# Sums of seven products built up in PSUM, with ScalarE copying between the products

## The chip, the cores and the metric

The kernel runs on one core of a Trainium2 chip. A core has a matrix engine (TensorE, in the profile PE, with its weight loads as PEld), three engines for elementwise work (VectorE as DVE, ScalarE as ACT, GpSimd as POOL), a queue engine (SyncE as SP) and 16 DMA engines. Matrix products land in PSUM, in banks of 128 partitions by 512 float32; everything else lives in SBUF. Each engine works through its own queue in order, and engines wait for one another by semaphores.

The metric is the time of one execution on the device in microseconds, as the median of the runs. Lower is better.

## The reference

x is 2048 x 512. It is normalised per row, and two branches use it:

```python
    x = A_x
    xn = _layernorm(x, axis=-1)
    s = _A_ref(xn, A_wqkv, A_wo)
    g = _silu(_B_ref(xn, B_w1, B_b1, B_w2, B_b2))
    return x + s * g
```

Branch A is attention with 32 heads of 16 channels: `qkv = x @ wqkv` (512 x 1536), then each position attends to 8 positions at distances 0, 2, ..., 14 behind it, with a softmax over the 8, and `@ wo` (512 x 512). Branch B is `relu(x @ w1 + b1) ** 2 @ w2 + b2` with 1792 hidden channels. Everything is float32.

## The kernel before

**Precision.** A float32 product is made of three passes in a faster format: each operand is split into a high and a low part, and high x high, high x low and low x high are added in PSUM (`PASSES`). ScalarE makes the high parts (`high`), VectorE or GpSimd the low ones (`low`). A product of 128 rows with a 256-deep half of the weights is thus 6 matmuls of 128 x 512, a full 512-deep projection 12.

**Stages.** The first stage takes the 16 tiles of 128 rows in pairs. It loads and normalises x, transposes it, splits it (`xt`), projects it to q, k and v and stores these to DRAM (`sq`, `sk`, `sv`). The second stage takes four chunks of 512 rows and, for each, the 14 slices of the hidden layer (`up`, `down`), with the output product of the attention (`out_product`) in between. The attention itself (products `pr` and `pv` with reductions) runs on VectorE beside both stages, as a stream of small steps that the function `pump` hands out.

**Order of the work.** Every engine keeps the order in which the program text calls it. A planner's clock counts priced work of PE and VectorE; `pump(margin)` issues attention steps while VectorE's clock stays below PE's plus a margin, and `not_before(t)` moves VectorE's clock forward where an operation is expected to wait. In the first stage, `plan` lists for each pair of tiles and each of six steps the preparation of later pairs (transposes, high and low parts, statistics, normalisation, loads), and `beside(a, step)` issues that step's list and then pumps.

**The pairs of seven products.** For the tile pairs starting at 4, 6, 8, 10 and 12 (`SEVEN`), q and k of both tiles a and b are computed from seven half-depth products in place of eight (a scheme of the Strassen and Winograd kind). With sums `S[a, 0..3]` of halves of x (made by `sums`, split by `high_sums` and `low_sums`) and sums T1 to T4 of weights, the products are called here by their weights:

- Q0 (first half of tile a), Q1 (second half of a), T1, T2, T3 (with S0, S1, S2), K1 (with S3), T4 (second half of b);
- q of a = Q0 + Q1; u2 = Q0 + T2; u3 = u2 + T3; q of b = u3 + T4; k of a = u2 + T1 + K1; k of b = u3 + T1.

`pair_of_seven(a)` issues them. Each product goes to a PSUM buffer of its own (`psA`, tag "acc", four banks shared with the v projections `qkv(·, 2)`). ScalarE copies two of them (Q0 and T1) into the staging tiles `stg` of q and k; VectorE adds the other five to `stg` straight from PSUM, and GpSimd makes two more additions from SBUF. Then `store_qkv` sends k and q to DRAM on SP's queue. In the profile these products are `pm`, the projections `pq`; nearly all instructions carry the line 87 of a recording helper.

Of the kernel before, what the change touches and what calls it, by code (L numbers as in the profile page):

```python
# [8 lines left out]
F32 = mybir.dt.float32  # L9
FR = mybir.dt.float32r  # L10
AF = mybir.ActivationFunctionType
# [3 lines left out]
P = 128  # L15
# [15 lines left out]
GR = 8  # L31
CH = D // GR
# [7 lines left out]
Q0, Q1, K0, K1, V0, V1, T1, T2, T3, T4 = range(10)  # L40
# [11 lines left out]
MATMUL, TRANSPOSE, DVE_FIXED, SHARED, SLACK, LATE, ROOM0, ROOM = 227, 150, 150, 200, 500, 3000, 500, 3500  # L52
# [5 lines left out]
def body(ctx: ExitStack, tc: tile.TileContext, x, wqkv, wo, w1, b1, w2, b2, out):  # L58
# [3 lines left out]
    clock = {"PE": 0.0, "V": 0.0}  # L62
# [28 lines left out]
    PE, V, A, G = Ordered(nc.tensor, "PE"), Ordered(nc.vector, "V"), Ordered(nc.scalar), Ordered(nc.gpsimd)  # L91

    def not_before(t):
        clock["V"] = max(clock["V"], t)
# [3 lines left out]
    def queue(out, in_):  # L98

        tc.keep_in_program_order(dma(out, in_))  # L100
# [10 lines left out]
    def psA(name):  # L111
        return psum.tile([P, 512], F32, name=name, tag="acc", bufs=4)
# [21 lines left out]
    px, pstg, pxT = (p1ctx.enter_context(tc.tile_pool(name=n, bufs=1)) for n in ("px", "pstg", "pxT"))  # L134
# [17 lines left out]
    def buffer(name, i):  # L152
        return wts.tile([P, 2, 2, 512], FR, name=name, tag=f"b{i}")


    wq = [buffer(f"wq{i}", i) for i in range(10)]
# [213 lines left out]
    def pump(margin=-SLACK):  # L370

        limit = clock["PE"] + margin
        flush(clock["PE"])
        while True:
            if coming[0] is None:
                coming[0] = next(stream, None)
            if coming[0] is None or clock["V"] + coming[0] > limit:
                break
            coming[0] = next(stream, None)
        if coming[0] is None:  # L380
            not_before(limit)
# [11 lines left out]
    def next_w():  # L393

        f = len(w12)
        if f < NF:
            w12[f] = buffer(f"w{f}", HOME[f]) if f in HOME else p2.tile([P, 2, 2, 512], FR, name=f"w{f}")
            for i, r in enumerate(raws.pop(f)):
                split(w12[f][:, 0, i], w12[f][:, 1, i], r, G)
            if f + 2 < NF:  # L400
                load_w(f + 2)
# [3 lines left out]
    mv, means, rs, shifts, xn, xb, pTs, xt, xT, seen, Sf, Sp = ({} for _ in range(12))  # L405
# [122 lines left out]
    def part_x(t, h):  # L528
        return lambda p, i: xt[t][:, p, 2 * h + i]

    def part_s(a, j):
        return lambda p, i: Sp[a, j // 2][:, p, j % 2, i]

    def product(a, n, lhs, w):

        ps = psA(f"pm{a}_{n}")
        k = 0
        for i in range(2):
            for p, q in PASSES:
                PE.matmul(ps, lhs(p, i), wq[w][:, q, i, :], start=k == 0, stop=k == 5)  # L540
                k += 1
        return ps.rearrange("p (g c) -> p g c", g=GR)

    def new_stg(t, s):
        stgs[s] = pstg.tile([P, GR, 2, CH], F32, name=f"stg{t}_{s}", tag="stg", bufs=4)

    def qkv(t, s, between=None, late=False):

        ps = psA(f"pq{t}_{s}")
        order = [(kt, a, b) for kt in range(KT) for a, b in PASSES]  # L550
        if late:
            order.sort(key=lambda o: o[1])
        for n, (kt, a, b) in enumerate(order):
            PE.matmul(ps, xt[t][:, a, kt], wq[2 * s + kt // 2][:, b, kt % 2, :], start=n == 0, stop=n == 11)
            if between and n == 5:
                between()
        evacuate(t, s, ps)

    def evacuate(t, s, ps):
        if t % 2 == 0:  # L560
            new_stg(t, s)
        A.activation(stgs[s][:, :, t % 2], ps.rearrange("p (g c) -> p g c", g=GR), AF.Copy)
        if t % 2:
            store_qkv(t, s)

    def store_qkv(t, s):
        r0 = (t - 1) * P + (0 if s == 0 else HALO)
        dst = (sq, sk, sv)[s][:, r0:r0 + UP, :].rearrange("g (p e) c -> p g (e c)", e=2)
        queue(dst, stgs[s].rearrange("p g e c -> p g (e c)"))
        done = done_tiles["qkv"[s]]  # L570
        done[0] = t + 1
        done[1][t // 2] = clock["PE"]
# [8 lines left out]
    def up(c, f):  # L581
        ph = psH(f"ph{c}_{f}")
        n = 0
        for kt in range(KT):
            for a, b in PASSES:
                PE.matmul(ph.rearrange("p (j n) -> p j n", n=P), w12[f][:, a, 0, kt * P:(kt + 1) * P],
                          xT[c][:, :, b, kt, :], start=n == 0, stop=n == 11)
                n += 1
        if f == NF - 1 and c + 1 < NCH:
            load_xT(c + 1)  # L590
        h = hpool.tile([P, 2, 512], FR, name=f"h{c}_{f}", tag="h", bufs=3)
        A.activation(ph, ph, AF.Relu, bias=b1t[:, f:f + 1])
        A.activation(h[:, 0], ph, AF.Square)

        pool = c or f < 2 or f > 11
        full = hpool.tile([P, 512], F32, name=f"hf{c}_{f}", tag="hf") if pool else ph
        A.activation(full, ph, AF.Square)
        if pool:
            G.tensor_sub(h[:, 1], full, h[:, 0].bitcast(F32))
        hs[f] = h, None if pool else ph, clock["PE"] + 2000  # L600

    def lowh(f):
        h, ph, t = hs[f]
        if ph is not None:
            not_before(t)
            V.tensor_sub(h[:, 1], ph, h[:, 0].bitcast(F32))
# [29 lines left out]
    ps = psA("pq0_1")  # L636
# [10 lines left out]
    stats(2)  # L647
    clock.update(PE=12000.0, V=12500.0)
    qkv(1, 1, None, True)
    lows(0, 2)  # L650
    norm(2)
    stats(3)
    constants()
    qkv(0, 0, lambda: highs(2, 0))
    trans(2)
    lows(2, 0)
    norm(3)
    stats(4)
    qkv(1, 0, lambda: highs(2, 2))
    trans(3)  # L660
    lows(2, 2)
# [38 lines left out]
    for a in range(2, NT, 2):  # L700
        n, t = (2 if a < 6 else 0), a + 2
# [29 lines left out]
    def beside(a, step):  # L731

        for f, args in plan.get((a, step), ()):
            f(*args)
        for n in range(ahead.get((a, step), 0)):
            next_w()
        pump(LATE)
# [15 lines left out]
    def pair_of_seven(a):  # L753

        b, last = a + 1, a + 2 == NT
        new_stg(a, 1)
        new_stg(a, 0)
        q, k = stgs[0], stgs[1]
        p = product(a, 1, part_x(a, 0), Q0)
        A.activation(q[:, :, 0], p, AF.Copy)  # L760
        p = product(a, 5, part_s(a, 0), T1)
        A.activation(k[:, :, 1], p, AF.Copy)
        beside(a, 0)
        p = product(a, 6, part_s(a, 1), T2)
        not_before(clock["PE"])
        V.tensor_add(k[:, :, 0], q[:, :, 0], p)
        p = product(a, 2, part_x(a, 1), Q1)
        beside(a, 1)
        not_before(clock["PE"])
        V.tensor_add(q[:, :, 0], q[:, :, 0], p)  # L770
        p = product(a, 7, part_s(a, 2), T3)
        not_before(clock["PE"])
        V.tensor_add(q[:, :, 1], k[:, :, 0], p)
        G.tensor_add(k[:, :, 0], k[:, :, 0], k[:, :, 1])
        G.tensor_add(k[:, :, 1], k[:, :, 1], q[:, :, 1])
        p = product(a, 3, part_s(a, 3), K1)
        beside(a, 2)
        qkv(a, 2)
        not_before(clock["PE"] - 12 * MATMUL)
        V.tensor_add(k[:, :, 0], k[:, :, 0], p)  # L780
        store_qkv(b, 1)
        beside(a, 3)
        p = product(a, 4, part_x(b, 1), T4)
        beside(a, 4)
        not_before(clock["PE"])
        V.tensor_add(q[:, :, 1], q[:, :, 1], p)
        store_qkv(b, 0)
        if last:
            for f in range(2):
                up(0, f)  # L790
                pump()
            lowh(0)
        qkv(b, 2)
        beside(a, 5)

    for a in range(2, NT, 2):
# [89 lines left out]
    for c in range(NCH):  # L886
# [4 lines left out]
        for f in range(2, NF):  # L891
# [6 lines left out]
            if c == 0 and f in (3, 6):  # L898

                i = f // 6  # L900
# [65 lines left out]
        else:  # L966
# [13 lines left out]
            for j in range(2, TPC):  # L980
                n = D // 2 if j == TPC - 1 else D
# [25 lines left out]
```

## Time and profile before

| | |
|---|---|
| runs, us | 492.69, 496.27, 496.73 |
| median, us | 496.27 |
| span of the profiled execution, us | 487.2 |
| TensorE busy, mean granted clock | 481.0 us (99%), 1.000 |
| VectorE, ScalarE, GpSimd busy | 437.9 us (90%), 220.0 us (45%), 242.7 us (50%) |
| HBM traffic over the span | 160 GB/s |

The profile is of one execution; only its span, from the first to the last instruction, is given, and the run times include what lies before and after it. Times in it are microseconds from the start of the span unless marked ns. The window of the pairs of seven products is from 42 to 119 us. Where a row of instructions ends in "<-", the engine stood idle before it until the named engine and tile released it. Matmuls overlap their neighbours, so the duration of one (389 ns) is longer than the distance between two.

### The profile page before, as it was taken

What the parts mean: (1) busy time and instruction counts of PE and PEld (TensorE: products, weight loads), DVE (VectorE), ACT (ScalarE), POOL (GpSimd) and SP (SyncE); (2) the same over time, 40 slices, a digit from 0 to 9 for tenths busy, and PEclk for the clock granted to TensorE, in tenths of its full rate; (3) what the DMA queues carried; (4) which work ended last, traced back from release to release, by engine and by line L of the source; (5) the groups of instructions that cost most, each with busy time, mean ns of one, the idle gap of its engine ahead of it and who ended that gap; (6) DMA issues with size and microseconds to landing.
All of it is one profiled execution on the core that took longest, in us unless ns stands there. A gap on an engine that the chain in (4) does not pass through costs nothing.

```text
span 487.2 us, 5957 instructions
## 1 busy us (share of the span) xinstructions
PE 481.0 (99%) x2124; PEld 395.4 (81%) x2124; DVE 437.9 (90%) x369; ACT 220.0 (45%) x392; POOL 242.7 (50%) x178
## 2 busy tenths in 40 slices
PE   8999999999999999999999999999999999999996
PEld 5887788888888888888888888888888888888886
DVE  5987999999999997999999999999999999989234
ACT  5556386523454657336612432652233366223331
POOL 1325244044657869367546426784643488352210
PEclk9999999999999999999999999999999999999999
DMA  8899999879938998274618337371924755030322
GB/s 281 219 249 278 302 289 278 215 210 315 289 87 221 264 194 229 77 233 76 170 45 209 82 64 262 60 200 31 226 48 85 248 93 152 16 108 23 86 86 88
DMA packets 65530, 81.47 MB, mean 167 GB/s; under 512 B 6108, under 2 KB 49372, under 8 KB 64732
## 3 DMA queue, kind: packets, MB, share of 16 engines
q1 hardware_dynamic: 61180, 54.87, 40.6%
q10 hardware_dynamic: 4320, 26.22, 21.3%
q8 instruction: 17, 0.28, 0.3%
q14 instruction: 13, 0.11, 0.1%
HBM read 50.60 MB, written 27.32 MB: 160 GB/s over the span
## 4 chain that ended last, share of the span: by engine, by line
PE 96%; DVE 1%; issue 1%; DMA 1%; POOL 0%; ACT 0%; POOLq 0%
PE pb L87 31%; PE ph L87 31%; PE pq L87 15%; PE pm L87 9%; PE pw L87 9%; DVE pr L87 1%; DMA x<-in_A_x 1%; PE pxT L87 0%; POOL stg L87 0%; DVE z L87 0%; ACT xn L87 0%; DVE Sf L87 0%; DVE st L87 0%; ACT S L87 0%; DVE stg L87 0%
## 5 line engine op out<-in xcount | busy, mean ns | idle before, releaser
L87 PE MATMUL pb<-w,h 128*128 128x512 f32 x672 | 160.6, 389 | 0.0
L87 PEld LDWEIGHTS pb<-w,h 128*128 128x128 f32 x672 | 126.1, 188 | 26.2
L87 POOL TENSOR_TENSOR h<-hf,h 128x512 fp32r<-128x512 f32 x46 | 83.8, 1822 | 104.4 <-ACT hf L87 95.3
L87 PE MATMUL ph<-xU,w 128*128 128x512 f32 x504 | 120.6, 389 | 0.0
L87 PEld LDWEIGHTS ph<-xU,w 128*128 128x128 f32 x504 | 94.6, 188 | 19.6
L87 ACT ACTIVATE ph<-ph,b1t 128x512 f32<-128x512 f32 x56 | 36.9, 659 | 136.8 <-PE ph L87 135.5
L87 DVE TENSOR_TENSOR pr<-k,q 128x2048 f32<-128x2048 f32 x32 | 81.4, 2543 | 0.6
L87 DVE TENSOR_TENSOR pv<-v,L 128x2048 f32<-128x2048 f32 x32 | 79.0, 2468 | 2.5 <-POOL L L87 2.0
L87 DVE TENSOR_REDUCE L<-pr 128x128 f32<-128x2048 f32 x32 | 73.2, 2286 | 0.9
L87 DVE TENSOR_REDUCE v<-pv 128x256 f32<-128x2048 f32 x32 | 73.0, 2281 | 0.8
L87 PE MATMUL pw<-wot,oT 128*128 128x512 f32 (+1 forms) x204 | 45.9, 376 | 0.0
L87 PE MATMUL pq<-wq,xt 128*128 128x512 f32 x192 | 45.5, 389 | 0.0
L87 PEld LDWEIGHTS pw<-wot,oT 128*128 128x128 f32 x204 | 36.8, 188 | 7.1
L87 PEld LDWEIGHTS pq<-wq,xt 128*128 128x128 f32 x192 | 36.0, 188 | 7.5
L87 PE MATMUL ph<-xT,w 128*128 128x512 f32 x168 | 40.3, 389 | 0.0
L87 PEld LDWEIGHTS ph<-xT,w 128*128 128x128 f32 x168 | 31.5, 188 | 6.5
L87 ACT ACTIVATE h<-ph 128x512 fp32r<-128x512 f32 x56 | 33.7, 601 | 1.8
L87 ACT ACTIVATE stg<-pq 128x512 f32<-128x512 f32 x28 | 16.6, 597 | 39.5 <-PE pq L87 39.5
L87 POOL TENSOR_TENSOR w<-w1r,w 128x512 fp32r<-128x512 f32 x14 | 25.6, 1830 | 16.0 <-ACT w L87 15.6
L87 ACT ACTIVATE hf<-ph 128x512 f32<-128x512 f32 x46 | 27.3, 594 | 8.9 <-POOL h L87 8.9
L87 PE MATMUL pq<-wq,xT 128*128 128x512 f32 x132 | 30.9, 393 | 0.0
L87 PE MATMUL pm<-wq,S 128*128 128x512 f32 x120 | 29.7, 394 | 0.3 <-ACT S L87 0.3
(82 smaller groups left out, 505.1 us busy)
## 6 DMA issues: line engine op xcount, KB each, us to landing
k<-sk ACTq DMA_DIRECT2D x8, 960.0 KB, 7.9
v<-sv ACTq DMA_DIRECT2D x8, 960.0 KB, 8.2
sx<-xt SPq DMA_DIRECT2D x12, 512.0 KB, 5.6
xU<-sx ACTq DMA_DIRECT2D x6, 1024.0 KB, 7.9
x<-in_A_x SPq DMA_DIRECT2D x16, 256.0 KB, 5.2
sk<-stg SPq DMA_DIRECT2D x8, 512.0 KB, 4.9
sq<-stg SPq DMA_DIRECT2D x8, 512.0 KB, 5.7
sv<-stg SPq DMA_DIRECT2D x8, 512.0 KB, 5.7
```

Source lines behind the costliest of these rows:

```text
L87: return tc.keep_in_program_order(f(*a, **k))
```

## The change

The sums are no longer formed by VectorE. Three PSUM buffers are taken at the start of a pair: `sums_ps`, `first` and `five`.

- `sums_ps` receives Q0. Then T2, T3 and T4 are accumulated into it, so that it holds Q0, u2, u3 and q of b in turn. ScalarE copies it after each: to the PSUM buffer `first`, to a new SBUF tile `u2`, to the q tile of b (u3) and again to the q tile of b.
- `first`, which holds the copy of Q0, has Q1 accumulated into it and is copied out as q of a.
- `five` receives T1, is copied to the k tile of b, and has K1 accumulated into it.
- VectorE keeps one addition, k of a = u2 + `five`; GpSimd keeps one, k of b += u3.

The order of the products changes from Q0, T1, T2, Q1, T3, K1, v of a, T4, v of b to Q0, T1, v of a, T2, Q1, first half of v of b, T3, K1, second half of v of b, T4. The planned steps 0 to 5 move with it; step 3 and the store of k now come in the middle of v of b, and q is stored last.

```diff
-    def product(a, n, lhs, w):
-        ps = psA(f"pm{a}_{n}")
+    def product(ps, lhs, w, start=True):
         k = 0
         for i in range(2):
             for p, q in PASSES:
-                PE.matmul(ps, lhs(p, i), wq[w][:, q, i, :], start=k == 0, stop=k == 5)
+                PE.matmul(ps, lhs(p, i), wq[w][:, q, i, :], start=start and k == 0, stop=k == 5,
+                          skip_group_check=True)
                 k += 1
+
+    def heads(ps):
         return ps.rearrange("p (g c) -> p g c", g=GR)
...
         q, k = stgs[0], stgs[1]
-        p = product(a, 1, part_x(a, 0), Q0)
-        A.activation(q[:, :, 0], p, AF.Copy)
-        p = product(a, 5, part_s(a, 0), T1)
-        A.activation(k[:, :, 1], p, AF.Copy)
+        sums_ps, first, five = (psA(f"pm{a}_{n}") for n in range(3))
+        u2 = pstg.tile([P, GR, CH], F32, name=f"u2_{a}", tag="u2")
+        product(sums_ps, part_x(a, 0), Q0)
+        A.activation(first, sums_ps, AF.Copy)
+        product(five, part_s(a, 0), T1)
+        A.activation(k[:, :, 1], heads(five), AF.Copy)
         beside(a, 0)
-        p = product(a, 6, part_s(a, 1), T2)
-        not_before(clock["PE"])
-        V.tensor_add(k[:, :, 0], q[:, :, 0], p)
-        p = product(a, 2, part_x(a, 1), Q1)
+        qkv(a, 2)
         beside(a, 1)
-        not_before(clock["PE"])
-        V.tensor_add(q[:, :, 0], q[:, :, 0], p)
-        p = product(a, 7, part_s(a, 2), T3)
-        not_before(clock["PE"])
-        V.tensor_add(q[:, :, 1], k[:, :, 0], p)
-        G.tensor_add(k[:, :, 0], k[:, :, 0], k[:, :, 1])
-        G.tensor_add(k[:, :, 1], k[:, :, 1], q[:, :, 1])
-        p = product(a, 3, part_s(a, 3), K1)
+        product(sums_ps, part_s(a, 1), T2, False)
+        A.activation(u2, heads(sums_ps), AF.Copy)
+        product(first, part_x(a, 1), Q1, False)
+        A.activation(q[:, :, 0], heads(first), AF.Copy)
         beside(a, 2)
-        qkv(a, 2)
-        not_before(clock["PE"] - 12 * MATMUL)
-        V.tensor_add(k[:, :, 0], k[:, :, 0], p)
-        store_qkv(b, 1)
-        beside(a, 3)
-        p = product(a, 4, part_x(b, 1), T4)
-        beside(a, 4)
-        not_before(clock["PE"])
-        V.tensor_add(q[:, :, 1], q[:, :, 1], p)
-        store_qkv(b, 0)
+
+        def seventh():
+            product(sums_ps, part_s(a, 2), T3, False)
+            A.activation(q[:, :, 1], heads(sums_ps), AF.Copy)
+            G.tensor_add(k[:, :, 1], k[:, :, 1], q[:, :, 1])
+            product(five, part_s(a, 3), K1, False)
+            not_before(clock["PE"])
+            V.tensor_add(k[:, :, 0], u2, heads(five))
+            store_qkv(b, 1)
+            beside(a, 3)
+
...
-        qkv(b, 2)
+        qkv(b, 2, seventh)
+        beside(a, 4)
+        product(sums_ps, part_x(b, 1), T4, False)
+        A.activation(q[:, :, 1], heads(sums_ps), AF.Copy)
+        store_qkv(b, 0)
         beside(a, 5)
```

In `qkv` the matmuls also get `skip_group_check=True`, since `seventh` is called between its sixth and seventh matmul.

More of the change, by code (lines that the diff above doesn't have):

```diff
@@ L553, in qkv @@
         for n, (kt, a, b) in enumerate(order):
-            PE.matmul(ps, xt[t][:, a, kt], wq[2 * s + kt // 2][:, b, kt % 2, :], start=n == 0, stop=n == 11)
+            PE.matmul(ps, xt[t][:, a, kt], wq[2 * s + kt // 2][:, b, kt % 2, :], start=n == 0, stop=n == 11,
+                      skip_group_check=True)
             if between and n == 5:
```

## The prediction

> **What bounds the kernel now.** I read the page first: the busy times and the slices.
>
> ```profile
> span 487.2 us, 5957 instructions
> PE 481.0 (99%) x2124; PEld 395.4 (81%) x2124; DVE 437.9 (90%) x369; ACT 220.0 (45%) x392; POOL 242.7 (50%) x178
> PE   8999999999999999999999999999999999999996
> PEclk9999999999999999999999999999999999999999
> ```
>
> TensorE (PE) is busy in every slice at the full granted clock, and the change leaves its matmuls as they are in number and size. VectorE (DVE), which the change relieves, is busy for 90%, but a busy engine need not be the bound, so the chain of waits came next.
>
> ```profile
> PE 96%; DVE 1%; issue 1%; DMA 1%; POOL 0%; ACT 0%; POOLq 0%
> 6.92 2.84 PE pq L87 x6
> ...
> 42.26 7.35 PE pm L87 x31
> ...
> 59.69 7.47 PE pm L87 x30
> ...
> 477.88 5.60 PE pw L87 x36
> ```
>
> The columns are start, length, what. From 6.92 to 477.88 + 5.60 = 483.48 us the chain is PE, except for one excursion between the rows at 42.26 and 59.69. The change touches neither the head (6.9 us) nor the tail (487.2 - 483.5 = 3.7 us). A gain can only come from PE time lost in between, so I asked for the five pairs of tiles that the change rewrites (tiles 4 to 13), one window each.
>
> ```profile
> 42.10:57.10 15.00, 15.00 (x66) 11.98 (x65) 13.50 (x15) 8.84 (x19) 5.84 (x9) 1.00 1.08 307
> 57.40:73.95 16.55, 16.10 (x68) 12.23 (x67) 15.41 (x27) 13.43 (x30) 6.55 (x14) 1.00 1.00 291
> 73.95:88.92 14.97, 14.97 (x68) 12.40 (x67) 13.77 (x21) 9.25 (x20) 4.45 (x8) 1.00 0.84 239
> 88.92:103.88 14.96, 14.96 (x67) 12.39 (x67) 14.02 (x19) 6.42 (x12) 5.28 (x4) 1.00 0.77 195
> 103.88:118.84 14.96, 14.96 (x67) 12.39 (x67) 13.15 (x18) 4.83 (x9) 5.13 (x4) 1.00 1.03 305
> 120.00:480.00 360.00, 360.00 (x1590) 298.07 (x1589) 331.23 (x204) 154.13 (x260) 202.06 (x112) 1.00 0.53 137
> ```
>
> After the stretch come the busy times of PE, weight load, DVE, ScalarE (ACT) and GpSimd (POOL), then the clock. By the code a pair has seven products of 6 matmuls and two v projections of 12: 66 matmuls, so 14.96 / 66 = 0.2267 us each, a product 1.36 us, a projection 2.72 us. Four pairs run at that pace, and from 120 to 480 us PE is busy throughout. Only the second pair (tiles 6 and 7) loses time: 16.55 - 14.96 = 1.6 us. The weight loads show what it waits for:
>
> ```profile
> 58.23 0.76 PEld L87 LDWEIGHTS pm<-wq,xt 128*128 128x128 f32 x4 [0.62 <-DVE xt L87]
> 59.68 0.30 PEld L87 LDWEIGHTS pm<-wq,S 128*128 128x128 f32 x2 [0.69 <-ACT S L87]
> 60.41 1.69 PEld L87 LDWEIGHTS pm<-wq,S 128*128 128x128 f32 x8 [0.43 <-DVE S L87]
> ```
>
> It waits for its own operands, which DVE and ACT prepare: 0.62 + 0.69 + 0.43 = 1.7 us of waiting, the 1.6 lost within its reading. So the ceiling of any gain is about 1.6 us of 487.2, or 0.3%.
>
> **The change, part by part.** Its work, per engine:
>
> ```profile
> L87 DVE TENSOR_TENSOR stg<-stg,pm 128x512 f32<-128x512 f32 x25 | 16.7, 682 | 4.3 <-PE pm L87 1.4 <-POOL stg L87 1.1 <-DMA sk<-stg 0.9
> L87 POOL TENSOR_TENSOR stg<-stg 128x512 f32<-128x512 f32 x5 | 6.5, 1292 | 29.4 <-DVE stg L87 22.4 <-ACT mean L87 3.9 <-issue 3.2
> L87 ACT ACTIVATE stg<-pm 128x512 f32<-128x512 f32 x10 | 5.8, 593 | 5.4 <-DMA sk<-stg 2.7 <-PE pm L87 1.9 <-DMA w2r<-in_B_w 0.8
> L87 ACT ACTIVATE ph<-ph 128x512 f32<-128x512 f32 x10 | 5.9, 594 | 0.0
> L87 ACT ACTIVATE ph<-ph,b1t 128x512 f32<-128x512 f32 x56 | 36.9, 659 | 136.8 <-PE ph L87 135.5 <-DVE pr L87 1.3
> ```
>
> DVE goes from 25 additions to 5: 20 x 0.682 = 13.6 us less. POOL goes from 10 to 5: 5 x 1.292 = 6.5 us less. ACT goes from 10 copies to 30: 20 x 0.593 = 11.9 us more, 2.4 us a pair. One new copy a pair goes from PSUM to PSUM. No row shows a plain copy of that kind; the square in place (ph<-ph) takes 0.594 and the form with a bias 0.659. I take 0.594, the nearer in operands; the other end adds 5 x 0.065 = 0.3 us on ACT. None of this is on PE. The DVE and POOL savings are worth nothing by themselves, because PE does not wait for those engines outside the second pair; the remaining DVE work (the attention) merely comes earlier.
>
> What counts are the new hand-overs PE, ACT, PE. One bank now takes four products in turn, and PE may add the next only when ACT has read the sum. In the new order of issue this stands between, in PE time: first sum to second product, T1 and a projection, 1.36 + 2.72 = 4.08 us; second to third, Q1 and half a projection, 2.72; third to fourth, K1 and the other half, 2.72. In the built program the second projection also reuses the bank of the first (T2 and Q1 between: 2.72), and the next pair's first projection in most pairs gets the bank of the last sum (Q0 and T1 between: 2.72). A hand-over costs one copy, 0.59, and the end of the last matmul, 0.389 by the next row against the 0.227 pace (0.16): 0.75 us.
>
> ```profile
> L87 PE MATMUL pb<-w,h 128*128 128x512 f32 x672 | 160.6, 389 | 0.0
> L87 DVE TENSOR_REDUCE L<-pr 128x128 f32<-128x2048 f32 x32 | 73.2, 2286 | 0.9
> ```
>
> So PE waits only when ACT is over 2.72 - 0.75 = 1.97 us late. ACT works strictly in the order of its queue, and in tiles 4 to 9 that queue holds the statistics of later tiles, ahead of the copies:
>
> ```profile
> 45.62 0.59 ACT L87 ACTIVATE mean<-x 128x512 f32<-128x512 f32 x1
> ...
> 47.14 1.06 ACT L87 ACTIVATE stg<-pm 128x512 f32<-128x512 f32 x2
> ...
> 59.00 0.63 ACT L87 ACTIVATE S<-Sf 128x512 fp32r<-128x512 f32 x1 [3.60 <-DVE Sf L87]
> ...
> 61.00 0.58 ACT L87 ACTIVATE stg<-pq 128x512 f32<-128x512 f32 x1
> ...
> 65.58 1.07 ACT L87 ACTIVATE xt<-pxT 128x512 fp32r<-128x512 f32 x2
> 66.53 0.39 ACT L87 ACTIVATE Sf<-pxT 128x256 f32<-128x256 f32 x1
> 66.80 0.83 ACT L87 ACTIVATE xn<-x,shift,rs 128x512 f32<-128x512 f32 x1
> ```
>
> A statistics block (mean to var, four instructions) is 47.14 - 45.62 = 1.5 us; the rest start 0.5 (copies, splits, S), 0.3 (Sf) and 0.7 us (normalisation, xn) apart. Walking the new queue with these durations:
> - First pair: ACT reaches its first copy at 47.14 as now and has it done at 47.73. PE has begun at 42.1 and wants T2 at 42.1 + 24 x 0.2267 = 47.5. Wait: 0.2 us.
> - Second pair, start: the operands come by the same DVE steps. Four additions leave the queue (2.7 us), and a reduction of 2.3 us (the row just above) moves ahead in it, as does the wait for K1. No gain; I keep the 1.6 us lost there.
> - Second pair, first projection: it wants the bank of the first pair's last sum. That copy stands behind S and one block, so it runs from 61.0 to 61.6; PE is ready at about 61.4. Wait: 0.2 us.
> - Second pair, later: two blocks, two normalisations, two splits and the copies fill ACT (13.43 + 2.4 = 15.8 us in the window). From the last copy at 61.0: copy and S 1.0, block 1.5, two copies 1.0, normalisation 0.7 make 65.2; the v copy, two splits, Sf and the other normalisation (0.5 + 1.0 + 0.3 + 0.7) make 67.7, so the copy ahead of T3 ends at 68.3. PE, let go at 61.6, wants it 30 matmuls later, at 68.4. No wait, with no room either.
> - Third pair: a block stands ahead of the copy before T3, which ends 9.7 us into the pair against 9.5 wanted. Wait: 0.2 us, of which I count 0.1.
> - Fourth and fifth pairs: ACT is busy 6.4 and 4.8 us of 15, no block left, no wait. The loads of the next attention inputs move up into ACT's queue in the fourth pair; the q load waits there for a store issued a pair earlier, which lands long before by this row:
>
> ```profile
> sq<-stg SPq DMA_DIRECT2D x8, 512.0 KB, 5.7
> ```
>
> The sum is 0.2 + 0.2 + 0.1 = +0.5 us on 487.2. Moved with the seventh step: the planned work beside it (splits for the next pair) is issued 1.36 us of PE time nearer to its use, and the store of k, then v, then q in SP's queue instead of k, q, v; only the second pair has no room for that, counted above. What is queued behind the last copy on ACT (the next pair's first copy) follows within 0.6 us against 4.08 of room. The last copy also waits for POOL's addition, 1.3 us, which can start a copy after T3, over 3 us ahead.
>
> The Trainium skill (Perfetto Trace Analysis, Matmuls) asks that independent matmul groups rotate through banks so that evacuation overlaps the next group, while one accumulation group stays in one bank. Read strictly, three bare hand-overs a pair would add 5 x 3 x 0.75 = 11 us; here other groups stand between them, so I expect the trace to side with +0.5.
>
> **The rivals.**
>
> (1) Slower: ACT's queue sets PE's pace. Place: the hand-overs of the second, third and fourth pairs. Price: with two blocks or a block, a split and a normalisation ahead of a copy, ACT is 2.7 to 2.9 us late, 0.7 to 0.9 over the 1.97 allowed; at three hand-overs in each of three pairs that is 9 x 0.7 = 6.3 us, 503 us in all. For it: ACT would have 15.8 us of work in 14.96. Against it: the walk above finds the blocks apart. It decides once ACT falls a second block behind. By the rule of the skill just named this is the side it would come out on.
>
> (2) Faster: the shorter DVE queue delivers the second pair's operands in time. Price: -1.6, 494.7 us. Against it: the wait for K1 stands in that queue.
>
> (3) Slower: the clock drops because PE pauses at each hand-over. Price: one pair at half clock, +15, 511 us. Against it: the second pair paused for 1.6 us and its window still shows 1.00. The skill (TensorE: Matmul & The Clock Gate, psum-queue depth-cycling) reports such a fall for a kernel that pauses between groups; this trace shows none.
>
> (4) The attention, issued earlier on DVE, stands ahead of a low part of h that PE needs. Price: one reduction, 2.3 us, 499 us; two or more are possible.
>
> That the change does not do what it says is excluded by the built order: one addition on DVE, one on POOL, six copies on ACT a pair.
>
> **How the numbers follow.** The three runs are 492.69, 496.27 and 496.73; the profiled span is 9.1 us below the median, launch and end that the page does not show. Adding 0.5 to the median gives 496.8. Chances: the forecast 0.72, rival 1 0.10, rival 2 0.10, rival 3 0.02, rival 4 0.06. Faster by over 1% (5 us, about what this kernel's runs can tell apart) would need more than all the PE time lost, so only 0.02 is left for it, out of the scatter of the runs. Slower by over 1%: rivals 1 and 3 and a sixth of rival 4, 0.13. Within 1%: the rest, 0.85. The range goes from the lowest run less the 1.6 of rival 2 (491.1, rounded to 491.5) to the highest run with the 0.5 and half of rival 1 (496.7 + 0.5 + 3.2, rounded to 500.5).
>
> **What would show it.** Right: DVE's additions from PSUM number 5 and ACT's copies 30; the windows of the five pairs stay at 15.0 to 15.3 us, the second at 16.5 to 17; from 120 to 480 us PE stays busy. Wrong: PE or its weight load waiting on an ACT copy for over 1 us in a pair (rival 1); a second pair of 15 us (rival 2); a clock below 1.00 in a window (rival 3); PE waiting for h after 130 us (rival 4).

## The result, and the profile after

| | before | after |
|---|---|---|
| runs | 12 | 12 |
| median, us | 492.69 | 495.55 |
| lowest and highest, us | 488.57, 496.73 | 492.38, 500.18 |
| ratio to before, 95% interval | 1 | 1.007 (1.0041 to 1.0098) |
| span of the first profile, us | 487.2 | 495.1 |

The changed kernel is slower by 2.9 us by the medians, and by 0.7%, about 3.4 us, by the ratio, which is formed without each kernel's slow runs. The forecast was +0.5 us, and within 1%. The two spans differ by 7.9 us, much more than the medians, so the first thing to settle is which part of that belongs to the change. Every run for which both numbers are known is 1.7 to 1.9 us longer than its span. The first profile of before, with a span of 487.2, is therefore a run of 489.0 us, one of the fastest of that kernel.

The page of after, busy times, slices and the chain of waits by engine:

```profile
span 495.1 us, 5947 instructions
PE 484.2 (98%) x2124; PEld 396.2 (80%) x2124; DVE 423.1 (85%) x349; ACT 229.0 (46%) x412; POOL 241.3 (49%) x173
PE   8999999999999999999999997999999999999997
...
PE 74%; DVE 11%; DMA 10%; issue 2%; ACT 1%; SPq 1%; POOL 1%; ACTq 0%; POOLq 0%; DVEq 0%
```

The work moved as planned: DVE has 20 instructions fewer, ACT 20 more, POOL 5 fewer. PE now has a hole in the 25th slice, at some 305 us, far behind the pairs that were edited, and of the chain that ended last, 96% PE before, a quarter now lies on other engines, most of it on DVE and DMA. The windows of the five pairs and of the stretch behind them, with the columns of before's table:

```profile
42.10:57.10 15.00, 14.92 (x65) 11.71 (x64) 12.88 (x13) 11.02 (x23) 4.54 (x8) 1.00 1.09 307
57.40:73.95 16.55, 15.81 (x66) 11.84 (x65) 10.45 (x21) 14.18 (x33) 5.22 (x12) 1.00 0.99 275
...
88.92:103.88 14.96, 14.96 (x68) 12.39 (x67) 12.74 (x20) 9.50 (x20) 4.71 (x3) 1.00 1.03 260
103.88:118.84 14.96, 13.99 (x62) 11.08 (x61) 10.34 (x10) 5.53 (x11) 1.18 (x1) 1.00 1.00 298
120.00:480.00 360.00, 356.38 (x1564) 294.10 (x1563) 322.00 (x194) 152.53 (x260) 206.88 (x114) 1.00 0.53 136
```

Two stretches lose that did not before: the fifth pair (0.97 us, and five matmuls fewer in it) and the second stage (3.6 us). The second pair loses 0.3 us more than it did (PE busy for 15.81 us in place of 16.10). What the weight loads wait for in the pairs:

```profile
45.26 2.59 PEld L87 LDWEIGHTS pq<-wq,xt 128*128 128x128 f32 x12 [0.52 <-ACT stg L87]
...
58.72 0.76 PEld L87 LDWEIGHTS pm<-wq,xt 128*128 128x128 f32 x4 [0.90 <-DVE xt L87]
60.16 0.30 PEld L87 LDWEIGHTS pm<-wq,S 128*128 128x128 f32 x2 [0.68 <-ACT S L87]
60.89 0.76 PEld L87 LDWEIGHTS pm<-wq,S 128*128 128x128 f32 x4 [0.43 <-DVE S L87]
62.10 2.60 PEld L87 LDWEIGHTS pq<-wq,xt 128*128 128x128 f32 x12 [0.45 <-ACT stg L87]
...
83.97 2.61 PEld L87 LDWEIGHTS pm<-wq,S 128*128 128x128 f32 x12 [0.22 <-ACT u L87]
...
113.81 1.23 PEld L87 LDWEIGHTS pq<-wq,xt 128*128 128x128 f32 x6 [1.40 <-ACT stg L87]
```

The waits at 62 and 84 us are hand-overs that the forecast named, each about twice its size. The one at 45 us is a hand-over too, but not the one named: the v projection, which the change moves forward, wants a bank whose copy ACT has behind a statistics block. The one at 113.81 is not in the forecast. ACT's rows tell what it is:

```profile
107.44 0.60 ACT L87 ACTIVATE stg<-pm 128x512 f32<-128x512 f32 x1 [0.78 <-PE pm L87]
113.16 0.60 ACT L87 ACTIVATE stg<-pq 128x512 f32<-128x512 f32 x1 [5.13 <-DMA sk<-stg]
```

ACT stands 5.1 us because the staging tile that it wants is still being stored: `sk` of the pair before, issued at 103.85 us, took 9.2 us to land (5.4 in before, where the same wait was 2.7 us and cost PE nothing). In after the loads of the next attention inputs (960 and 512 KB) are issued at 97.9 and 98.5 us, ahead of that store, and land 8.9 and 10.5 us later, while it is under way; in before they came at 108.6 and 109.2. The rows of the two queues, first of after, then of before:

```profile
97.93 0.53 ACTq L87 DMA_DIRECT2D k<-sk  x1
...
98.50 0.62 ACTq L87 DMA_DIRECT2D q<-sq  x1
...
103.85 0.38 SPq L100 DMA_DIRECT2D sk<-stg  x1
```

```profile
103.10 0.39 SPq L100 DMA_DIRECT2D sk<-stg  x1
...
108.58 0.60 ACT L87 ACTIVATE stg<-pm 128x512 f32<-128x512 f32 x1 [2.66 <-DMA sk<-stg]
108.60 0.53 ACTq L87 DMA_DIRECT2D k<-sk  x1
109.17 1.00 ACTq L87 DMA_DIRECT2D q<-sq  x1
```

The loads moved because the planner's clock no longer counts the additions, so that the attention is handed out earlier in the built program, by 28 matmuls on the mean over its reductions, loads and stores.

The hole at 305 us, on PE and on ACT's queue:

```profile
298.64 5.60 PE L87 MATMUL pb<-w,h 128*128 128x512 f32 x24
307.35 7.17 PE L87 MATMUL ph<-xU,w 128*128 128x512 f32 x24 [3.11 <-issue]
```

```profile
291.87 0.52 SPq L323 DMA_DIRECT2D so<-v  x1
...
293.40 2.92 ACTq L87 DMA_DIRECT2D xU<-sx  x2
```

The matmuls that wait read `xU`, the next chunk's x. The second half of its load stood in ACT's queue until a store of the attention, issued at 291.87 us, had landed (in the built program the load waits for that transfer, eight before it in the order of issue). The 24 matmuls behind the pause take 7.17 us where the 24 ahead of it take 5.60, and from 300 to 310 us the granted clock is 0.85: the pause costs 3.1 us and 1.6 more by the clock.

Are these two places the 3.4 us? One profile of a kernel whose runs scatter over 8 us cannot say, so experiments follow.

### The profile page after: what moved, and what is told of

Its sections match the earlier page's. It is cut to its first block, busy times and chain, and to the rows that moved or that the text cites. A ratio compares the mean times of both kernels' runs of the same rounds, so it can differ in the third digit from the quotient of the medians.

```text
span 495.1 us, 5947 instructions
## 1 busy us (share of the span) xinstructions
PE 484.2 (98%) x2124; PEld 396.2 (80%) x2124; DVE 423.1 (85%) x349; ACT 229.0 (46%) x412; POOL 241.3 (49%) x173
## 4 chain that ended last, share of the span: by engine, by line
PE 74%; DVE 11%; DMA 10%; issue 2%; ACT 1%; SPq 1%; POOL 1%; ACTq 0%; POOLq 0%; DVEq 0%
PE pb L87 26%; PE ph L87 26%; PE pw L87 9%; PE pq L87 6%; PE pm L87 6%; DVE L L87 3%; DVE pr L87 3%; DMA x<-in_A_x 2%; DMA v<-sv 2%; DMA sk<-stg 2%; DMA sq<-stg 2%; DVE pv L87 1%; DMA so<-v 1%; DVE v L87 1%; DMA sx<-xt 1%
## 5 line engine op out<-in xcount | busy, mean ns | idle before, releaser
L87 POOL TENSOR_TENSOR h<-hf,h 128x512 fp32r<-128x512 f32 x46 | 76.0, 1652 | 107.8 <-ACT hf L87 105.6
L87 PE MATMUL ph<-xU,w 128*128 128x512 f32 x504 | 122.1, 393 | 3.1 <-issue 3.1
L87 PEld LDWEIGHTS ph<-xU,w 128*128 128x128 f32 x504 | 95.6, 190 | 23.5 <-issue 3.5
L87 DVE TENSOR_TENSOR pr<-k,q 128x2048 f32<-128x2048 f32 x32 | 79.2, 2475 | 0.6
L87 PE MATMUL pq<-wq,xt 128*128 128x512 f32 x192 | 46.8, 391 | 1.1 <-ACT stg L87 1.0
L87 POOL TENSOR_TENSOR w<-w1r,w 128x512 fp32r<-128x512 f32 x14 | 23.4, 1671 | 23.5 <-ACT w L87 23.5
```

The costliest lines, as they stand in the source:

```text
L87: return tc.keep_in_program_order(f(*a, **k))
```

## The experiments

Theory 1: the attention, issued earlier, costs the time through late stores and loads. Theory 2: the hand-overs between PE and ACT cost it. Theory 3: four staging tiles are too few. Theory 4, in one expectation, puts the late store of k down to GpSimd's addition. Each run is compared with before on the same chip.

**The attention later (late_attention).** After, with its additions counted again:

```diff
+        def counted():
+            not_before(clock["PE"])
+            clock["V"] += 512 / 0.96 + DVE_FIXED
+
```

`counted()` is called behind the copies of u2, of q of a, of u3 and of q of b, four times a pair.

> After's products and copies are kept; the planner's clock counts 683 ns of DVE for each of the four removed additions again, so that the loads and steps of the attention are handed out about as late as in before. Theory 1 (the time went because the attention stream moved earlier): the waits of PE in the fifth pair (1.4 us of weight load waiting for ACT's copy) and the pause of 3.1 us at 304 us with its lower clock both go; 120 to 480 us is PE busy for 359 us or more; the span is that of before's profile plus 0.8, 488.0, and the time about 2.5 us under after's. Theory 2 (the new hand-overs between PE and ACT cost it): the first three pairs start as late as in after, and the time stays within 0.5 us of after's. Theory 4 (POOL's addition behind the weight splits holds up the store of k): the wait in the fifth pair stays, at 1 us of PE or more, and only the pause at 304 us goes.

This was meant to put the attention back to about where before has it. In the built programs it does not: the attention's steps come 43 matmuls later than in before on the mean, and 70 later than in after. So what follows is the time of a new place of the attention, not of the old one.

Measured: 488.52 us (7 runs, 488.22 to 489.16), ratio to before 0.9908 (0.9876 to 0.994). Faster than both kernels, by more than theory 1 allowed, and with a scatter of 1 us where before has 8. Both holes are gone, and with the wait in the fifth pair theory 4 goes too, since the edit leaves GpSimd's addition as it is:

```profile
42.10:57.10 15.00, 14.91 (x66) 11.90 (x65) 10.69 (x14) 11.28 (x24) 4.34 (x7) 1.00 1.09 301
57.40:73.95 16.55, 16.21 (x72) 13.09 (x71) 10.62 (x17) 15.35 (x36) 7.44 (x13) 1.00 1.01 305
120.00:480.00 360.00, 360.00 (x1592) 298.25 (x1591) 336.99 (x205) 154.27 (x259) 198.03 (x113) 1.00 0.53 139
```

PE is busy from 120 to 480 us, and the window of the second pair holds 72 matmuls in place of 66. DVE's rows ahead of the second pair say why, first of after, then of late_attention:

```profile
55.18 0.69 DVE L87 TENSOR_TENSOR stg<-u,pm 128x512 f32<-128x512 f32 x1 [0.81 <-PE pm L87]
55.79 2.28 DVE L87 TENSOR_REDUCE L<-pr 128x128 f32<-128x2048 f32 x1
57.98 0.68 DVE L87 TENSOR_TENSOR xt<-pxT,xt 128x512 fp32r<-128x512 f32 x1
```

```profile
54.74 0.69 DVE L87 TENSOR_TENSOR stg<-u,pm 128x512 f32<-128x512 f32 x1 [2.98 <-PE pm L87]
55.35 0.68 DVE L87 TENSOR_TENSOR xt<-pxT,xt 128x512 fp32r<-128x512 f32 x1
```

The low part of x that PE waits for stands behind a reduction of the attention in after and in front of it in late_attention, 2.6 us earlier. The hand-overs stay. The one ahead of T3 in the second pair, which the forecast had "with no room", now takes 0.76 us:

```profile
67.21 2.59 PEld L87 LDWEIGHTS pm<-wq,S 128*128 128x128 f32 x12 [0.76 <-ACT u L87]
```

**The xU load as one transfer (one_xu_load).**

```diff
-        for j in range(0, TPC, 2):
-            A.dma_start(xT[c][:, j:j + 2].bitcast(F32), sx[c][:, j:j + 2])
+        A.dma_start(xT[c].bitcast(F32), sx[c])
```

> After, with the load of a chunk's x (xU) as one DMA instead of two halves. Theory 1: the pause at 304 us comes from the second half, which waits for the store of v of an attention unit issued eight transfers earlier; as one DMA the load waits only for an old weight load, so the pause of 3.1 us and the 1.7 us of lower clock behind it go, the window from 300 to 310 us has PE busy for 10 us at a clock of 1.00, and the median falls by 2 to 4 us (not every run of after has the pause). The fifth pair keeps its wait of 1.4 us. Rival (the load is late because the DMA engines are busy with the attention's loads, not because it is issued late): a pause of 1 us or more stays, and the time is within 1 us of after's.

**A fifth staging tile (five_staging)**: `bufs=4` becomes `bufs=5` for the tag "stg". **Both (both_mends).**

> After, with five staging tiles for the sums instead of four. Theory 3 (in the fifth pair ACT's copy of v waits 5.1 us for the store of k to leave its staging tile): the wait goes, and with it the 1.4 us of weight load waiting in that pair and the lateness of DVE that costs 1.2 us at 187 to 192 us; the pause at 304 us stays; the span falls by 2 to 3 us. Rival (the wait only moves to the next tile, since the stores land 9 us after issue): another staging wait of over 2 us on ACT in the fifth pair, and no change of the span.

> After, with five staging tiles and the load of xU as one DMA. Theory 1 with 3: both places are gone, what is left is the 0.8 us of new hand-overs in the first three pairs, so the span is about 488 us and the time 4 to 6 us under the profiled one of after, within 1 us of before's. Theory 2: the time stays within 1 us of after's median.

Measured: 495.48 us and ratio 1.0041 (1.001 to 1.0073) for one_xu_load, 495.05 and 1.0033 (1.0001 to 1.0065) for five_staging, 493.83 and 1.0018 (0.9987 to 1.005) for both. In one_xu_load the pause at 304 us is gone, as expected (PE is busy for 10.00 us from 300 to 310 us, at a clock of 1.00), but PE waits for a low part of h from POOL three times instead, 0.97, 1.04 and 0.95 us at 226, 315 and 403 us, so the expected fall of 2 to 4 us did not come. In five_staging the fifth pair runs full (14.96 of 14.96 us) and ACT's longest wait for a staging tile is 1.0 us, although the store of k still takes 9 us to land; two waits for h, which were expected to go, remain with 0.86 and 0.52 us, and so does a pause for xU, shorter than in after:

```profile
304.81 5.73 PE L87 MATMUL ph<-xU,w 128*128 128x512 f32 x24 [1.52 <-issue]
```

The profile of both_mends has neither long pause, but five waits for h, 0.4 to 1.2 us each, and one of 0.25 us for xU (PE is busy for 356.18 us from 120 to 480 us), where only the 0.8 us of hand-overs were expected to be left. So theory 3's wait is real: ACT waits 5.1 and 3.6 us with four tiles and 1.0 and 1.1 us with five. But by the ratios the mends gain 1.4 and 1.8 us, and 2.6 together, and the intervals overlap after's. One_xu_load also shows that PE does not lose by the staging wait in every run: with four tiles, ACT waited 3.6 us there and PE not at all.

**The additions of before not counted (before_early), and before with a later attention (before_late); late_attention later still (later_attention).** In before_early the clock is put back behind the four additions that the change takes off VectorE, and the `not_before` ahead of each goes with it; the additions themselves are made as before. The other two add 2 us of clock a pair:

```diff
         (pair_of_seven if a in SEVEN else pair)(a)
+        if a in SEVEN:
+            clock["V"] += 2000
```

> Before, with nothing of the change but this: the four additions of a pair that the change takes from VectorE are no longer counted by the planner's clock (they are still made there). The attention's steps are then issued some 20 to 60 matmuls earlier than in after, as after's are some 30 earlier than before's. Theory 1 (the time went because the attention is issued earlier): this alone makes before as slow as after or slower, 0.5 to 2% over before, with waits of PE for h, for the fifth pair's staging tiles or for xU behind the stores of the attention. Theory 2 (the new hand-overs between PE and ACT cost it): none of them is here, so the time stays within 0.3% of before's.

> Before, with 2 us added to the planner's VectorE clock after each of the five pairs, which puts the attention's steps within a few matmuls of where late_attention has them (its 23rd reduction at matmul 1360 against 1362). Theory 1: before gains what late_attention gained, a time of 488 to 489.5 us, within 1 us of late_attention's 488.5, and little scatter; the products' accumulation in PSUM is then worth nothing. Rival (the gain of late_attention over before comes from the additions that left VectorE, whose queue before still has): the time stays at 491 us or more.

> Late_attention with 2 us more on the planner's VectorE clock after each pair: the attention's steps come another 30 to 80 matmuls later. Theory 1 with a best place: the slack is used up, the time is that of late_attention within 1 us (487.5 to 489.5) as long as the last attention units are still done before the last chunk wants them; past that point PE waits for the attention's output at the end (450 us and later) and the time rises by 2 us or more. Rival (late_attention's gain came from one lucky place of a few transfers): the time goes back to 492 us or more, with waits as in after.

Measured: before_early 502.33 us, ratio 1.0172 (1.0113 to 1.0231); before_late 509.39, 1.035 (1.0306 to 1.0395); later_attention 564.44, 1.1484 (1.1424 to 1.1543). The first shows that issuing the attention earlier can cost time with no hand-over in sight, at a place some 30 matmuls ahead of after's; some 6 us of it lie in the pairs, where DVE's operands and the staging tiles come late:

```profile
108.17 2.58 PE L87 MATMUL pm<-wq,S 128*128 128x512 f32 x10 [0.93 <-DVE S L87]
115.87 1.66 PE L87 MATMUL pm<-wq,S 128*128 128x512 f32 x6 [2.40 <-ACT stg L87]
```

There is a cliff on the late side. Before_late is 20 us above theory 1's range. It does not stand at late_attention's place: its steps come 15 matmuls later on the mean, the stores of the attention's output 5 matmuls ahead to 25 behind. In later_attention the wait that the expectation named for a place too late did come, but it costs 75 us, and from 257 us on, not only at the end. PE waits for the attention's output, first in before_late, then in later_attention:

```profile
426.22 5.48 PE L87 MATMUL pw<-wot,oT 128*128 128x512 f32 x12 [4.23 <-DVE oT L87]
```

```profile
257.48 5.49 PE L87 MATMUL pw<-wot,oT 128*128 128x512 f32 x12 [10.43 <-DVE oT L87]
```

**Before once more (before_again).**

> The kernel before, unchanged, for a second profile of it. The profile that the prediction used had a span of 487.2 us, 489 us of time, one of before's fastest runs; its median is 493 to 494. Theory 1: a usual run of before has pauses of PE in the second phase of the same kinds as after's (PE waits for h, or for xU), 3 to 7 us in sum, and a span of 490 to 494; before too issues its attention too early. Rival (the scatter lies at the start, where the clock comes up late in some runs, or outside of the span): PE is busy for 359 us or more from 120 to 480 us here too, and the first pair starts 2 us later than in the other profile, or the time is over 4 us longer than the span.

Measured: 494.0 us (10 runs, 488.16 to 495.99). The profile is of a usual run, span 492.8, and bears theory 1 out as to the pauses:

```profile
225.24 2.56 PE L87 MATMUL pb<-w,h 128*128 128x512 f32 x10 [0.53 <-POOL h L87]
236.90 2.60 PE L87 MATMUL pb<-w,h 128*128 128x512 f32 x10 [0.48 <-POOL h L87]
243.41 3.02 PE L87 MATMUL pw<-wot,oT 128*128 128x512 f32 x12 [1.19 <-DVE oT L87]
315.63 2.56 PE L87 MATMUL pb<-w,h 128*128 128x512 f32 x10 [0.75 <-POOL h L87]
404.76 2.56 PE L87 MATMUL pb<-w,h 128*128 128x512 f32 x10 [1.79 <-POOL h L87]
```

A usual run of before has holes in the second stage too, as many microseconds as after has (PE is busy for 355.25 us of 120 to 480 us, 356.38 in after). The first profile happened to be a run without them.

**The same place of the attention, with and without the change.** The insertion shown above with 700 and 1,500 ns in before, 1,000 and 2,000 ns in after. Within each pair of kernels the attention's stores are issued at the same matmuls; its other steps differ by 3 to 4 on the mean. After_plus10 has the attention 5 matmuls later than before, so it is the run that puts it back. The "third theory" of these expectations is a new one, a gain by the accumulation in PSUM, and not that of the staging tiles.

> Before, with 0.7 us added to the planner's VectorE clock after each of the five pairs: the attention's steps come 9 matmuls later than in before on the mean, and its stores of the output go out at the same matmuls as in after_plus10 (671, 908, 1097, 1280, 1470, 1657, 1853, 1950). Theory 1: the place of the attention sets the time, so this and after_plus10 agree within 1 us, after_plus10 being later by the 0.8 us of new hand-overs at most; both lie between 488 and 495 us. Theory 2 (the new hand-overs cost the 3 us): after_plus10 is 2 us or more slower than this one.

> After, with 1 us added to the planner's VectorE clock after each of the five pairs: the attention's stores go out at the same matmuls as in before_plus10. Theory 1: within 1 us of before_plus10, and 2 us or more under after. Theory 2: 2 us or more over before_plus10. A third theory (the accumulation in PSUM is a gain by itself, since it takes 13.6 us off VectorE, and the planner's clock only hid it): 2 us or more under before_plus10.

> Before, with 1.5 us added after each pair: the attention comes 29 matmuls later than in before, its stores at the same matmuls as in after_plus29 (692, 908, 1101, 1285, 1498, 1678, 1885, 1988), 14 matmuls ahead of late_attention's place on the mean. Theory 1: equal to after_plus29 within 1 us, and nearer to late_attention's 488.5 than to before_late's 509.4, since its stores lie 15 to 40 matmuls ahead of before_late's: 487.5 to 493 us. Theory 2: 2 us or more under after_plus29. Third theory: 2 us or more over after_plus29.

> After, with 2 us added after each pair: the attention's stores at the same matmuls as in before_plus29. Theory 1: within 1 us of before_plus29, 488 to 493 us. Theory 2: 2 us or more over before_plus29. Third theory: 2 us or more under before_plus29.

Measured: 493.49 against 496.02 us, and 493.40 against 495.27; ratios to before 1.0055 (1.0025 to 1.0085) against 1.0106 (1.0059 to 1.0153), and 1.0048 (1.0015 to 1.0081) against 1.0108 (1.0051 to 1.0166). With the attention's stores in the same place the change still costs 2.5 and 1.9 us by the medians. In the first pair of kernels the runs hardly overlap (492.59 to 495.10 against 494.82 to 496.63 us), in the second they do (492.24 to 495.23 against 493.92 to 499.95). Theory 2 asked for 2 us or more, which the first pair shows and the second just misses. And neither after_plus10 nor after_plus29 came out 2 us under after, as theory 1 had it. So theory 1 falls as the cause of what the change costs, save for the staging wait, which does not hold up PE in these two profiles. The gain by the accumulation does not show at these two places; at late_attention's place no kernel without the change was run. The second stage of each pair of kernels shows the same holes at the same places, for instance 1.77 us in both kernels of the first pair:

```profile
314.25 3.53 PE L87 MATMUL pb<-w,h 128*128 128x512 f32 x10 [1.77 <-POOL h L87]
```

```profile
315.50 3.87 PE L87 MATMUL pb<-w,h 128*128 128x512 f32 x10 [1.77 <-POOL h L87]
```

The difference is made earlier. The table splits each profile at two rows, the first product of the first pair and the first matmul of the second stage (`ph<-xT`; 126.83 us in before, 129.03 in after):

| kernel | the five pairs, to the second stage, us | from there to the end, us |
|---|---|---|
| before, first profile | 84.7 | 360.4 |
| before_again | 84.2 | 366.7 |
| before_plus10, before_plus29 | 84.1, 84.1 | 365.9, 365.0 |
| after | 87.0 | 366.1 |
| five_staging, one_xu_load, both_mends | 85.0, 85.0, 85.1 | 364.5, 365.2, 366.3 |
| after_plus10, after_plus29 | 85.6, 85.6 | 365.6, 364.6 |
| late_attention | 84.1 | 361.1 |
| before_early, before_late | 90.6, 84.9 | 367.9, 379.9 |

In the usual run the change costs 0.8 to 1.5 us in the pairs, and 1.4 to 2 more where the staging tile comes late (after's 87.0 against 85.0 to 85.6). The rows of the weight loads say what this consists of. In five_staging and one_xu_load they wait 2.7 us in the pairs, in the usual runs of before (before_again, before_plus10, before_plus29) 1.7 to 1.8. New are 0.46 and 0.22 us for ACT's copies, the hand-overs; and the low part of x in the second pair is waited for 0.89 us in place of 0.37 to 0.48, in after because of the reduction ahead of it. In after, after_plus10 and after_plus29 the 0.5 us of the first pair's v projection come on top.

Behind the pairs, the usual run takes 364.5 to 367 us with the change and without it. Late_attention is the exception: its pairs take what before's usual ones take (84.1), and its gain lies behind them (361.1, as in the fast first profile of before with 360.4).

**What the holes of the second stage hang on.** At the end of a chunk ACT copies four banks (`z<-pb`), POOL adds to the copies and then makes the low part of the next chunk's h. The load of v for the next attention unit (`v<-sv`) stands somewhere in ACT's queue around these copies, and it waits for the store of the last unit. In before_again it stands ahead of them, in late_attention behind:

```profile
213.48 0.54 ACTq L87 DMA_DIRECT2D v<-sv  x1
214.07 2.07 ACT L87 ACTIVATE z<-pb 128x512 f32<-128x512 f32 x4 [8.88 <-DMA so<-v]
```

```profile
211.12 2.64 ACT L87 ACTIVATE z<-pb 128x512 f32<-128x512 f32 x4 [6.18 <-PE pb L87]
...
221.43 0.54 ACTq L87 DMA_DIRECT2D v<-sv  x1
```

Measured from the start of the last product of the chunk (the row of 23 or 24 matmuls `pb`), the copies start after 3.6 us at all three chunk ends of late_attention, and PE loses nothing. In before's first profile they start after 5.0 to 5.1 us, and PE loses nothing. In before_again they start after 6.3, 6.5 and 7.6 us, and PE waits 0.5, 0.75 and 1.8 us for h soon after; in before_plus29 once after 8.5 us, with a wait of 2.7. That is read from the profiles (all but later_attention's), not tried by moving that one load. One chunk end speaks against it (after's first, 6.9 us and no wait), and it doesn't cover all: before_early loses 1.5 and 3.7 us with copies on time, both times behind a step of the attention of 3.0 to 3.1 us that stands ahead of POOL's additions.

## Why the prediction was right, and where not

**The number.** The forecast of +0.5 us within 1% held as to the 1%, but the change costs 2.9 to 3.4 us, six to seven times as much. That the time forecast, 496.8 us, lies so near the measured 495.55 is luck: it was added to a median of three runs, 496.27, and over twelve runs before's median is 492.69.

**The bound and the ceiling.** PE is busy for 96 to 99% of the span in every kernel but later_attention (89%), and the work taken off VectorE and GpSimd did not pay by itself, as forecast: after_plus10 and after_plus29 have the shorter queues and are slower than their partners. The ceiling of 1.6 us was read from a run without holes in the second stage and was too low: the usual run of before loses 4.75 us of PE time from 120 to 480 us, and late_attention gains 4.5 us on before.

**The costs of the operations.** 5 additions left on DVE, 30 copies on ACT; the copy from PSUM to PSUM takes 0.58 us (0.594 forecast). ACT's walk was nearly right: the first copy ran from 47.15 us (47.14 forecast), the one at which PE waits in the second pair ended at 62.05 (61.6; S came later), the one ahead of T3 there at 68.65 (68.3), with no wait, as forecast.

**The hand-overs, +0.5 us.** The mechanism was right and the size too small: 0.45 us for the second pair's projection and 0.22 in the third pair, against 0.2 and 0.1. In the first pair T2 did not wait; the projection ahead of it did, 0.52 us. That makes 0.7 us in the profiles without this last wait and 1.2 in those with it. On the rule of the Trainium skill that the prediction names, the trace sides with the smaller number: three bare hand-overs a pair would have been 11 us. The Trainium skill's advice (Perfetto Trace Analysis, Matmuls) to let independent groups rotate through the banks is what this kernel follows, and the price left is that of the places where ACT comes later than the other group lasts.

**The second pair, "no gain; I keep the 1.6 us".** Right as to the gain, and for the reason given: a reduction moved ahead of the low part of x. But that part now comes later than in before, 0.90 us of waiting in place of 0.62, so a loss was left out: 0.3 us against that profile, 0.4 to 0.5 against the usual runs. Late_attention shows the other case, rival 2: with that reduction later, those operands come on time, and the hand-overs are paid for.

**The step that failed: "fourth and fifth pairs: no block left, no wait", and the loads that move up dismissed by the q load's own wait.** What the walk left out is what the earlier loads do to others: 1.5 MB of them in front of the store of k, which lands 9.2 us after issue instead of 5.4, and a staging tile is not free when ACT wants it. Five_staging shows that the tile is the wait; that the loads are why the store is late is read from the times of issue and landing, and not tried. This is the term that the sum lacked, 1.4 us of waiting in the profile of after, and none for PE in that of one_xu_load.

**"From 120 to 480 us PE stays busy."** It failed in after (356.38 us of 360), and the same test fails in an ordinary run of before (355.25). The mistake is in the first section of the prediction: the profiled span was taken for what every run does, and 9.1 us between it and the median were put down to launch and end. What a run takes beyond its span is 1.7 to 1.9 us; the rest was that the profile showed one of the fastest runs.

**The rivals.** (1) The sign given for it came, a weight load waiting over 1 us for an ACT copy (1.40 us in the fifth pair), but not its mechanism: ACT was not behind in its queue, it waited for a store. (2) did not happen in after, and did in late_attention. (3) did not happen where it was placed: the windows of the pairs show 1.00. The clock fell at a chunk end, to 0.85 over 10 us behind a pause of 3.1 us, and 1.6 us were lost by it. (4) happened, small: 0.93 us of weight load waiting for h at 187 us, where a product and a reduction of the attention stand ahead of that low part.

**What the 0.7% consists of.** In the profile of after the pairs take 2.3 to 2.9 us more than in those of before (87.0 against 84.1 to 84.7): the hand-overs, the later low part of x and the staging wait. The stretch behind them is no longer than in a usual run of before. That fits the 2.9 us between the medians, but it is one profile, and the staging wait is not in every run.

**Open:** why after_plus10 and after_plus29 stay 1.9 to 2.5 us behind their partners by the medians, where the pairs account for 1.5; whether the hand-overs alone make up the loss, since no run takes them out and keeps the rest; and what in late_attention's place of the attention brings its gain. It was not tried step by step, and whether the accumulation in PSUM has a part in it is not known either.

## What to carry to other kernels

Where a planner hands out side work by a clock of priced operations, moving an operation to an engine that the clock does not count moves all the side work, here by 28 matmuls. Look up the new place in the built program, also behind a mend that is meant to restore the old one. The old place was no cure here: after_plus10, with the attention 5 matmuls from it, is no faster than after. A place 43 matmuls later than before's gave about 7 us over after, but the good stretch is narrow: some 15 matmuls earlier that gain is gone, in before_plus29 and in after_plus29, and some 15 later before_late loses 17 us.

Look for loads that wait for a store and stand in an engine's queue ahead of a copy that the bound engine needs next: in before_again and before_plus29 the copies behind such a load came 2.7 to 4.9 us later than in late_attention. And profile the kernel before twice when its runs scatter more than the effect looked for: a wait that is missing from one fast profile is no evidence that the usual run lacks it.

## What the hardware showed beside this

A subtraction of 128x512 from SBUF on POOL took 1.25 to 1.30 us alone and 3.3 us while DVE ran a product of two 2048-wide SBUF operands, and that product took 3.45 us, where the fastest of its kind took 2.23; DVE's reductions, with one operand, stayed at 2.29:

```profile
220.60 3.45 DVE L87 TENSOR_TENSOR pr<-k,q 128x2048 f32<-128x2048 f32 x1
224.08 2.29 DVE L87 TENSOR_REDUCE L<-pr 128x128 f32<-128x2048 f32 x1
```

```profile
221.86 3.33 POOL L87 TENSOR_TENSOR h<-hf,h 128x512 fp32r<-128x512 f32 x1
225.90 1.30 POOL L87 TENSOR_TENSOR h<-hf,h 128x512 fp32r<-128x512 f32 x1 [0.71 <-ACT hf L87]
```

Both tables are of before_again. The Trainium skill (GPSIMD Engine Reference, Specifications) says that GpSimd shares its SBUF interfaces with VectorE and contends with VectorE instructions that have two SBUF inputs; the rows agree. These 2 us come on top of the late copies at that chunk end, where PE waits 0.53 us for this low part of h.

The granted clock can fall behind a single pause of PE: to 0.85 over 10 us (300 to 310 us) around the pause of 3.1 us in after, and to 0.949 as the mean of later_attention, which pauses for up to 10.5 us at a time. The length of the pause does not decide it alone. Behind 1.77 us in before_plus10 the clock was 0.72 from 314 to 320 us, behind 1.79 us in before_again it was 1.00 from 404 to 410 us. The Trainium skill (TensorE: Matmul & The Clock Gate, psum-queue depth-cycling) tells of such a change of clock for a kernel that idles briefly and often between groups; here it is seen behind single pauses.

The first six matmuls of the kernel took 4.76 us instead of 2.84 in both_mends (4.69 in before_plus29), which puts all that follows 2 us later in these runs. The clock recorded for that stretch is 1.00, and why they are slow is open.
